# Loading x as runs of 112 consecutive rows in a fused causal convolution and SoLU layer

## The chip, the cores and the metric

The kernel runs on one core of a Trainium2 chip, in one launch. A core has four compute engines, each with its own queue of instructions that it works off strictly in order: TensorE (PE, matrix products into PSUM), VectorE (DVE), ScalarE (ACT) and GpSimd (POOL). A fifth queue, SyncE (SP), computes nothing: here it issues all DMAs, in order, and the DMAs run on 16 DMA engines. Engines wait for each other through semaphores. The metric is the device time of one execution in microseconds, the median over runs.

## The reference

x has 8 sequences of 4160 tokens with 192 features. Each of 8 heads (24 features) takes a causal convolution over 7 tokens with softmax weights, zero ahead of a sequence's first token. The result goes, token by token, through a feed-forward layer with 1024 hidden features.

```python
x_pad = np.concatenate([np.zeros((B, 6, D)), x], axis=1)
out = np.einsum('hk,bskhg->bshg', softmax(weight), windows_of_7(x_pad))
x = out.reshape(B * S, D)                       # 33280 tokens x 192
h = x @ w_in                                    # 192 -> 1024
solu = h * softmax(h)
ln = (solu - mean(solu)) / sqrt(var(solu) + 1e-6) * g_ln
return ln @ w_out                               # 1024 -> 192
```

## The kernel before

**Tiles.** The 33280 tokens are 260 tiles of 128. For each tile PE makes ph (128 x 1024, L815 and L838) from the convolved and transposed tokens yT; DVE takes the row minimum of the scaled ph (L869), ACT the exponential (L876), DVE the product (L886), ACT a half-precision copy p (L894) and the squares (L898), POOL the rest that the copy left out (L906). SP then issues a DMA that transposes p to pT (L908), PE multiplies pT by w_out into po (L938), five tiles after the tile's own ph, DVE brings po to SBUF (L948), POOL scales the rows (L1017), and SP stores them (L1030).

**Chunks.** The convolution works on chunks of 16 or 18 tiles (the first three chunks, `Chunk`, have another shape and are not touched by the change). Class `Strips` holds the other 14. A chunk's x comes in four loads (`load`, j = 0 to 3) into two SBUF tiles, one for the first half of the chunk's tokens ("late" 0) and one for the second ("late" 1). Even chunks and odd chunks use two sets of such tiles: one is named xs in the profile, the other xr. A load fetches strips of 48 rows: 32 tokens and the 16 ahead of them. 48 rows go to partitions 0 to 47 (half 0) or 64 to 111 (half 1), and 16 such strips, 64 tokens apart, lie side by side (18 in the last two chunks). Partitions 48 to 63 and 112 to 127 of these tiles are filled with zeros once, at the start (`clear`, L453: two DMAs for each of the four tiles).

**The maximum.** `sum_squares` (L376) is a reduction on DVE that takes the largest magnitude over all 128 partitions of half the strips of one tile, four per chunk. The convolution needs a scale, worked out from these four. Since a reduction reads both halves, it needs two loads to have landed.

**The first tokens of a sequence.** Where a strip starts with a sequence's first token, its 16 rows ahead belong to another sequence. `load` zeroes them with a memset on POOL right after it issued the load (L364); this memset waits for the load to land. It happens seven times, each time in xs.

**The product.** `product` (L400) runs, for each of two heads, eight matmuls of 48 rows by 32 output columns. They use both row halves of the array and its four column groups, so that all eight stand beside each other.

**The order.** It is written by hand. From tile 8 on, `three_steps` emits three tiles at a time: at the head of a step come the step's loads, then PE's products; a first "peak" (the maximum) stands on DVE ahead of the step's first row minimum L869, further ones at the end of the step. `chores` says at which tile k of chunk ch what is due: convolutions of chunk ch+1 at k = 0, 3, 6, 9; loads of chunk ch+3 at 12, 13 and 15, its fourth load at k = 1 of the next chunk; the four maxima of chunk ch+2 at 1, 4, 7 and 10. The lines are:

```python
if c2:
    fixed("load", (1, 2, 4, 5) if late else (-1, -1, -1, 1), [(c2, j) for j in range(4)])
    fixed("peak", (7, 8, 10, 12) if late else (1, 4, 7, 10), ...)
if c3:
    fixed("load", [q + late for q in (12, 13, 15 - late)], [(c3, j) for j in range(3)])
```

As 16 tiles are no multiple of three, the steps stand differently in each chunk; every third chunk they stand alike.

Of the kernel before, what the change touches and what calls it, by code (L numbers as in the profile page):

```python
# [9 lines left out]
F32 = mybir.dt.float32  # L10
# [9 lines left out]
def kernel(  # L20
# [34 lines left out]
    ROWS = HALO + Q  # L55

# [44 lines left out]
    def total(parts, name, bank=None):  # L101

        n = parts.shape[1]
        if bank is None:
            bank = single(f"pt_{name}")
        nc.tensor.matmul(
            bank[:, 512 - n : 512], ones, parts, start=True, stop=True
# [29 lines left out]
    class Chunk:  # L137
# [84 lines left out]

        def square_peaks(self):

            if self.peaks < self.cols:
                q = self.part[:, self.peaks : self.cols]
                act.activation(q, q, AF.Square, scale=16.0)

        def add_up(self, bank=None):
            self.tp = total(self.part[:, 0 : self.cols], f"x{self.ch}", bank)  # L230
# [99 lines left out]
    class Strips(Chunk):  # L330


        def __init__(self, ch):
# [3 lines left out]
            self.np, self.convs = 4, 0  # L337
# [6 lines left out]
        def place(self, j):  # L344
            half, late = j % 2, j // 2
            return half, late, strips[(self.ch - OLD) % 2][late][:, 0 : self.nt, :]

        def load(self, j):

            half, late, t = self.place(j)  # L350
            self.raw[j] = t
            assert self.ch < OLD + 2 or chunks[self.ch - 2].convs == 4
            nt, own = self.nt, slice(64 * half, 64 * half + ROWS)
            first = self.t0 + late * nt * P // 2 + Q * ((half + late) % 2) - HALO
            nc.sync.dma_start(
                t[own],
                bass.AP(
                    tensor=x.tensor, offset=first * D,
                    ap=[[D, ROWS], [2 * Q * D, nt], [1, D]],
                ),  # L360
            )
            for w in range(nt):
                if (first + HALO + 2 * Q * w) % S == 0:
                    pool.memset(t[64 * half : 64 * half + HALO, w, :], 0.0)  # L364

        def halves(self, j):
            late, n = j // 2, self.nt // 2
            return [(2 * late, j, j % 2 * n, (j % 2 + 1) * n)]

        def sum_squares(self, j, col, a, z):  # L370
            if self.part is None:
# [3 lines left out]
            self.sums += 1  # L375
            dve.tensor_reduce(  # L376
                self.part[:, col : col + 1], self.raw[j][:, a:z, :], AX.XY,
# [6 lines left out]
        def product(self, h, n, a, z, bank=None):  # L384
# [9 lines left out]
            for j in range(n):  # L394
                for half, c in STRIPS:
                    late, own = (half + c) % 2, slice(64 * half, 64 * half + ROWS)
                    raw = strips[(self.ch - OLD) % 2][late][own, 0 : self.nt, :].rearrange(
                        "p (t g) d -> p g t d", g=2
                    )
                    nc.tensor.matmul(  # L400
                        pc[late][Q * c : Q * (c + 1), :, j * HD : (j + 1) * HD],
                        taps[own, h + j, 64 * half : 64 * half + Q],
                        raw[:, c // 2, :, (h + j) * HD : (h + j + 1) * HD],
# [1253 lines left out]
```

## Time and profile before

| | us |
|---|---|
| three runs | 1296.66, 1298.22, 1305.03 |
| median | 1298.22 |
| the profiled execution, its own time | 1300.94 |
| its span, first to last instruction | 1299.2 |
| its PE clock, mean granted share | 0.955 |

All rows of the profile are of that one execution. A row of a group has its busy time, the mean of one in ns and the idle time of its engine ahead of it with what ended it. A row of a window has the busy time and count of each engine in a stretch, then the granted PE clock, the share of time that DMA packets took (of 16 engines; over 1 where packets overlap) and the GB/s moved. A row of the timeline has start, duration, engine, line, operation and, in brackets, the idle time ahead of it and what ended that. A DMA on SP's queue shows the time to issue it, not to run it.

### The profile page before, as it was taken

What the parts mean: (1) busy time and instruction counts of PE and PEld (TensorE: products, weight loads), DVE (VectorE), ACT (ScalarE), POOL (GpSimd) and SP (SyncE); (2) the same over time, 40 slices, a digit from 0 to 9 for tenths busy, and PEclk for the clock granted to TensorE, in tenths of its full rate; (3) what the DMA queues carried; (4) which work ended last, traced back from release to release, by engine and by line L of the source; (5) the groups of instructions that cost most, each with busy time, mean ns of one, the idle gap of its engine ahead of it and who ended that gap; (6) DMA issues with size and microseconds to landing.
All of it is one profiled execution on the core that took longest, in us unless ns stands there. A gap on an engine that the chain in (4) does not pass through costs nothing.

```text
span 1299.2 us, 24145 instructions
## 1 busy us (share of the span) xinstructions
PE 1154.4 (89%) x8854; PEld 665.9 (51%) x8854; DVE 994.1 (77%) x1736; ACT 954.8 (73%) x1613; POOL 756.3 (58%) x748
## 2 busy tenths in 40 slices
PE   5967877997989899798989979899896989999998
PEld 3644434554545455455445545455463555555556
DVE  8865666877868797787858868687886768878777
ACT  7954656786868688687767858677785777888786
POOL 3615453684656654766655746557556465676674
PEclk9997889998989999899989989899998899999999
DMA  8689999999999999999999999999999999999988
GB/s 230 124 125 163 151 195 177 201 174 189 195 182 204 172 201 183 179 196 187 204 159 185 188 181 196 171 195 188 183 198 156 193 179 194 201 162 182 184 148 181
DMA packets 736181, 235.69 MB, mean 181 GB/s; under 512 B 649230, under 2 KB 734654, under 8 KB 736062
## 3 DMA queue, kind: packets, MB, share of 16 engines
q1 hardware_dynamic: 736062, 234.15, 103.6%
q8 instruction: 69, 1.13, 0.4%
q14 instruction: 50, 0.41, 0.1%
HBM read 40.50 MB, written 25.56 MB: 51 GB/s over the span
## 4 chain that ended last, share of the span: by engine, by line
PE 42%; DMA 17%; POOL 15%; issue 12%; DVE 7%; ACT 4%; SPq 3%; DVEq 0%; POOLq 0%; ACTq 0%
PE po L938 20%; PE ph L815 17%; POOL p L906 10%; DMA pT<-p 9%; DMA xs<-in_x_dram 4%; DVE ph L869 3%; DMA xr<-in_x_dram 3%; PE ph L838 2%; SPq L908 2%; PE pc L400 2%; POOL raw L1017 2%; ACT p L894 2%; POOL t L1009 2%; DVE y L287 1%; DVE e L886 1%
## 5 line engine op out<-in xcount | busy, mean ns | idle before, releaser
L906 POOL TENSOR_TENSOR p<-e,p 128x1024 f16<-128x1024 f32 x257 | 546.8, 2135 | 387.2 <-ACT p L894 378.9
L938 PE MATMUL po<-ohl,pT 128*128 128x192 f16 (+1 forms) x4264 | 573.2, 293 | 119.5 <-DMA pT<-p 67.7
L938 PEld LDWEIGHTS <-pT 128*128 128x128 f16 x4264 | 397.0, 101 | 303.3 <-DMA pT<-p 85.0
L815 PE MATMUL ph<-whi,yT 128*128 128x512 f16 x1548 | 421.4, 381 | 3.8 <-DVE e L886 2.6
L876 ACT ACTIVATE e<-ph,sm 128x1024 f32<-128x1024 f32 x260 | 289.6, 1114 | 178.6 <-DVE ph L869 143.1
L886 DVE SCALAR_TENSOR_TENSOR e<-ph,cv,e 128x1024 f32<-128x1024 f32 x259 | 331.4, 1280 | 61.7 <-ACT e L876 61.0
L869 DVE TENSOR_SCALAR_CACHE_REDUCE ph<-ph,cv 128x1024 f32<-128x1024 f32 x259 | 332.8, 1287 | 35.6 <-PE ph L838 27.6
L894 ACT CAST p<-e 128x1024 f16<-128x1024 f32 x257 | 266.7, 1038 | 69.8 <-DVE e L886 50.2
L815 PEld LDWEIGHTS <-yT 128*128 128x128 f16 x2064 | 193.1, 98 | 238.1 <-issue 40.4
L898 ACT ACTIVATE sq<-e 128x1024 f32<-128x1024 f32 x260 | 274.1, 1054 | 0.2
L948 DVE TENSOR_REDUCE raw<-po 128x192 f32<-128x384 f32 x247 | 137.0, 555 | 71.5 <-PE po L938 71.4
L815 PE MATMUL ph<-wlo,yT 128*128 128x512 f16 x516 | 154.6, 382 | 0.0
L278 ACT ACTIVATE y<-pc,s 128x384 f16<-128x384 f32 (+7 forms) x158 | 72.3, 518 | 76.5 <-PE pc L400 60.9
L287 DVE SCALAR_TENSOR_TENSOR y<-pc,s,y 128x384 f16<-128x384 f32 (+7 forms) x158 | 82.0, 537 | 55.1 <-ACT y L278 54.7
L1017 POOL TENSOR_SCALAR raw<-raw,t 128x192 f32<-128x192 f32 x240 | 99.0, 425 | 0.0
L838 PE MATMUL ph<-wlo,yT 64*128 64x512 f16 x269 | 74.1, 380 | 0.6 <-DMA yT<-y 0.6
L376 DVE TENSOR_REDUCE xa<-xs 128x1 f32<-128x1536 f32 (+1 forms) x28 | 49.5, 1773 | 30.1 <-DMA xs<-in_x_dram 21.7
L376 DVE TENSOR_REDUCE xa<-xr 128x1 f32<-128x1536 f32 (+1 forms) x28 | 49.6, 1773 | 29.0 <-DMA xr<-in_x_dram 29.0
L838 PE MATMUL ph<-wlo,y 64*128 64x512 f16 x251 | 68.5, 380 | 1.5 <-DMA y<-yT 1.5
L364 POOL MEMSET xs<- 16x192 f32 x7 | 1.7, 247 | 103.7 <-DMA xs<-in_x_dram 92.1
L1009 POOL TENSOR_TENSOR t<-t,mhalf 128x8 f32<-128x8 f32 (+2 forms) x33 | 53.5, 1622 | 2.6
L876 ACT ACTIVATION_READ_ACCUMULATOR e<-ph,sm 128x1 f32 x260 | 50.1, 193 | 0.0
(142 smaller groups left out, 482.3 us busy)
## 6 DMA issues: line engine op xcount, KB each, us to landing
out_dram<-raw SPq DMA_DIRECT2D x127, 192.0 KB, 3.0
xs<-in_x_dram SPq DMA_DIRECT2D x24, 576.0 KB, 8.7
xr<-in_x_dram SPq DMA_DIRECT2D x24, 576.0 KB, 8.4
pT<-p SPq DMA_TRANSPOSE x263, 4.6
y<-yT SPq DMA_DIRECT2D x12, 256.0 KB, 3.4
xr<-in_x_dram SPq DMA_DIRECT2D x6, 480.0 KB, 5.8
xs<-in_x_dram SPq DMA_DIRECT2D x4, 648.0 KB, 9.0
xr<-in_x_dram SPq DMA_DIRECT2D x4, 648.0 KB, 8.6
```

What stands on the lines that cost most here:

```text
L376: dve.tensor_reduce(self.part[:, col : col + 1], self.raw[j][:, a:z, :], AX.XY, ALU.max, apply_absolute_value=True,)
L815: nc.tensor.matmul(bank, lhs, w[:, r, n * 512 : (n + 1) * 512], start=start and j == 0, stop=stop and j == len(ops) - 1,)
L838: nc.tensor.matmul(banks_of(t)[n], y[q, t.off : t.off + P], wlo[q, 1, n * 512 : (n + 1) * 512], start=start, stop=not start,)
L869: dve.tensor_scalar(t.ph, t.ph, t.cv[:, 0:1], None, ALU.mult, ALU.min, accum_out=t.bias)
L876: act.activation(t.e, t.ph, AF.Exp, bias=t.bias, scale=-1.0, accum_out=grp.z[:, g : g + 1])
L886: dve.scalar_tensor_tensor(t.e, t.ph, t.cv[:, 3:4], t.e, ALU.mult, ALU.mult, accum_out=t.grp.s1[:, t.g : t.g + 1],)
L894: act.copy(t.p16[:, :, 0, :], t.halves)
L898: act.activation(junk, t.e, AF.Square, accum_out=t.grp.s2[:, t.g : t.g + 1])
L906: eng.tensor_tensor(t.p16[:, :, 1, :], t.halves, t.p16[:, :, 0, :], ALU.subtract)
L938: nc.tensor.matmul(t.po[:, 0:n], t.pT[:, a, :], w, start=j == 0, stop=j == len(ops) - 1)
L948: dve.tensor_reduce(t.grp.raw[:, t.g, :], t.po[:, 0 : 2 * D].rearrange("p (a d) -> p d a", a=2), AX.X, ALU.add,)
L1017: pool.tensor_scalar(o, o, u, 1.0, ALU.mult, ALU.mult)
```

## The change

The loads of `Strips` change their shape. One load now takes 112 consecutive rows (`SPAN`) to partitions 0 to 111 at one go, and the next 112 rows start 128 tokens on. Rows 0 to 47 of such a run are one strip, rows 64 to 111 the strip 64 tokens later; rows 48 to 63 are x's rows between them, and no longer zeros. A chunk of 16 tiles has loads of 8, 8, 9 and 9 runs. The second class (late 1) starts 64 tokens earlier and has one run more, so that its row half 1 serves the strips that half 0 serves in the first class: all eight places in the array are still in use. The end of x doesn't fill a run: there two loads are cut, and their last run is zeroed first (a DVE memset that the DMA waits for).

With it go the fills (`clear`) and their eight DMAs; the maximum reads 112 partitions and one load alone; its four columns hold 8, 8, 9 and 9 tiles' worth; the first rows of a sequence are zeroed on DVE directly ahead of that load's maximum, no longer on POOL. Loads of chunk ch+3 are due at 13 and 14, its other two at k = 0 and 1 of the next chunk; the maxima at 3, 6, 8 and 10.

```diff
     class Strips(Chunk):
+        rows = SPAN
...
         def load(self, j):
 
-            half, late, t = self.place(j)
-            self.raw[j] = t
...
-            first = self.t0 + late * nt * P // 2 + Q * ((half + late) % 2) - HALO
+            late, q = divmod(j, 2)
+            m = self.nt // 2
+            n = m + late
+            self.raw[j] = t = strips[(self.ch - OLD) % 2][late][:, q * n : (q + 1) * n]
+            first = self.t0 + Q * q - HALO + late * (m * P - P // 2)
+            rows = min(SPAN, B * S - first - (n - 1) * P)
+            part = rows < SPAN
+            if part:
+                dve.memset(t[:, n - 1, :], 0.0)
+                nc.sync.dma_start(
+                    t[0:rows, n - 1, :],
...
             nc.sync.dma_start(
-                t[own],
+                t[0:SPAN, 0 : n - part],
                 bass.AP(
                     tensor=x.tensor, offset=first * D,
-                    ap=[[D, ROWS], [2 * Q * D, nt], [1, D]],
+                    ap=[[D, SPAN], [P * D, n - part], [1, D]],
                 ),
             )
-            for w in range(nt):
-                if (first + HALO + 2 * Q * w) % S == 0:
-                    pool.memset(t[64 * half : 64 * half + HALO, w, :], 0.0)
+            self.starts[j] = [
+                t[64 * half : 64 * half + HALO, w, :]
+                for half in range(2) for w in range(n)
+                if (first + 64 * half + HALO + P * w) % S == 0
+            ]
 
         def halves(self, j):
-            late, n = j // 2, self.nt // 2
-            return [(2 * late, j, j % 2 * n, (j % 2 + 1) * n)]
+            return [(j, j, 0, self.nt // 2 + j // 2)]
...
             self.sums += 1
+            for t in self.starts[j]:
+                dve.memset(t, 0.0)
             dve.tensor_reduce(
-                self.part[:, col : col + 1], self.raw[j][:, a:z, :], AX.XY,
+                self.part[0:SPAN, col : col + 1], self.raw[j][0:SPAN, a:z, :], AX.XY,
...
-                for half, c in STRIPS:
-                    late, own = (half + c) % 2, slice(64 * half, 64 * half + ROWS)
...
+                for q, late, half in STRIPS:
+                    own, skip = slice(64 * half, 64 * half + ROWS), late * (1 - half)
+                    c = Q * (2 * (half ^ late) + q)
                     nc.tensor.matmul(
-                        pc[late][Q * c : Q * (c + 1), :, j * HD : (j + 1) * HD],
+                        pc[late][c : c + Q, :, j * HD : (j + 1) * HD],
                         taps[own, h + j, 64 * half : 64 * half + Q],
-                        raw[:, c // 2, :, (h + j) * HD : (h + j + 1) * HD],
+                        self.raw[2 * late + q][
+                            own, skip : skip + m, (h + j) * HD : (h + j + 1) * HD
+                        ],
...
-    STRIPS = [(0, 0), (1, 1), (0, 2), (1, 3), (0, 1), (1, 0), (0, 3), (1, 2)]
+    STRIPS = [(q, late, half) for q in range(2) for late in range(2) for half in range(2)]
...
-    def clear(k, late):
-
-        for half in range(2):
-            nc.sync.dma_start(
-                strips[k][late][64 * half + ROWS : 64 * (half + 1)],
-                zero.unsqueeze(1).broadcast_to([64 - ROWS, NTM, D]),
             )
...
-                fixed("load", (1, 2, 4, 5) if late else (-1, -1, -1, 1), [(c2, j) for j in range(4)])
-                fixed("peak", (7, 8, 10, 12) if late else (1, 4, 7, 10),
+                fixed("load", (1, 2, 4, 5) if late else (-1, -1, 0, 1), [(c2, j) for j in range(4)])
+                fixed("peak", (7, 8, 10, 12) if late else (3, 6, 8, 10),
...
-                fixed("load", [q + late for q in (12, 13, 15 - late)], [(c3, j) for j in range(3)])
+                fixed("load", (13, 14), [(c3, 0), (c3, 1)])
```

Where instructions move. SP's queue near the end of chunk 4 (tiles 58 to 61), before. The names are the tiles above: pT with its transpose, xs with a load, out_dram with a store; "48x16x192" is partitions, strips and features.

```order
L908 DMA_TRANSPOSE pT_3434<-p_58_3431 128x16x128
L355 DMA xs_419<-in_x_dram 48x16x192 x2
L1030 DMA out_dram<-raw_2733 128x2x192
L908 DMA_TRANSPOSE pT_3503<-p_59_3500 128x16x128
L908 DMA_TRANSPOSE pT_3535<-p_60_3532 128x16x128
L908 DMA_TRANSPOSE pT_3574<-p_61_3571 128x16x128
L355 DMA xs_420<-in_x_dram 48x16x192
```

The same place in the changed kernel:

```order
L912 DMA_TRANSPOSE pT_3424<-p_58_3421 128x16x128
L366 DMA xs_417<-in_x_dram 112x8x192
L1034 DMA out_dram<-raw_2723 128x2x192
L912 DMA_TRANSPOSE pT_3491<-p_59_3488 128x16x128
L912 DMA_TRANSPOSE pT_3523<-p_60_3520 128x16x128
L912 DMA_TRANSPOSE pT_3562<-p_61_3559 128x16x128
L366 DMA xs_417<-in_x_dram 112x8x192
L366 DMA xs_418<-in_x_dram 112x9x192
```

For this chunk the loads come two, one and one before, and one, two and one now (the last is further on). In the other two standings of the steps they are two and two now. The transposes keep their order among each other.

DVE at the turn to the fourth chunk (tile 32), before. raw<-po is L948 of the text above, xa is the maximum, y the convolution's result on its way out of PSUM, ph the row minimum:

```order
L948 TENSOR_REDUCE raw_1875<-po_2007 128x192
L376 TENSOR_REDUCE xa_2075<-xs_419 128x1
L287 SCALAR_TENSOR_TENSOR y_73<-pc_6_0_2034,s_1846,y_73 128x8x48
L869 TENSOR_SCALAR ph_2025,sm_2078<-ph_2025,cv_1186 128x1024
L287 SCALAR_TENSOR_TENSOR y_73<-pc_6_1_2035,s_1846,y_73 128x8x48
L869 TENSOR_SCALAR ph_2052,sm_2083<-ph_2052,cv_1186 128x1024
```

In the changed kernel, from the same row minimum on (the two rows ahead of it are raw<-po and y, with no maximum between them):

```order
L873 TENSOR_SCALAR ph_2014,sm_2065<-ph_2014,cv_1178 128x1024
L290 SCALAR_TENSOR_TENSOR y_73<-pc_6_1_2024,s_1836,y_73 128x8x48
L873 TENSOR_SCALAR ph_2041,sm_2070<-ph_2041,cv_1178 128x1024
L890 SCALAR_TENSOR_TENSOR e_2068,s_32_1989<-ph_2014,cv_1178,e_2068 128x1024
L952 TENSOR_REDUCE raw_1863<-po_2081 128x192
L890 SCALAR_TENSOR_TENSOR e_2072,s_32_1989<-ph_2041,cv_1178,e_2072 128x1024
L873 TENSOR_SCALAR ph_2042,sm_2137<-ph_2042,cv_1178 128x1024
L952 TENSOR_REDUCE raw_1863<-po_2120 128x192
L890 SCALAR_TENSOR_TENSOR e_2139,s_32_1989<-ph_2042,cv_1178,e_2139 128x1024
L952 TENSOR_REDUCE raw_1863<-po_2153 128x192
L389 MEMSET xs_417 16x192
L390 TENSOR_REDUCE xa_2222<-xs_417 112x1
```

The maximum that stood ahead of tile 32's row minimum now stands a step (three tiles) later, with the memset that POOL had directly ahead of it.

POOL at the same turn, before (raw<-raw,t is L1017, cv the scales that the row minimum reads):

```order
L906 TENSOR_TENSOR p_28_1849<-e_1838,p_28_1849 128x2x512
L364 MEMSET xs_419 16x192
L1017 TENSOR_SCALAR raw_1480<-raw_1480,t_16_1039 128x192 x2
L906 TENSOR_TENSOR p_29_1921<-e_1914,p_29_1921 128x2x512
L218 TENSOR_SCALAR cv_1847<-cv_1847 128x1 x3
```

And changed:

```order
L910 TENSOR_TENSOR p_28_1839<-e_1828,p_28_1839 128x2x512
L1021 TENSOR_SCALAR raw_1470<-raw_1470,t_16_1031 128x192 x2
L910 TENSOR_TENSOR p_29_1909<-e_1902,p_29_1909 128x2x512
L219 TENSOR_SCALAR cv_1837<-cv_1837 128x1 x3
L910 TENSOR_TENSOR p_30_1942<-e_1906,p_30_1942 128x2x512
```

POOL's queue is the same but for the memset, which is gone from between two tiles' L906.

More of the change, by code (lines that the diff above doesn't have):

```diff
@@ L55 @@
     ROWS = HALO + Q
+    SPAN = 64 + ROWS
     QS = 2.0**-14
@@ L106, in total @@
         nc.tensor.matmul(
-            bank[:, 512 - n : 512], ones, parts, start=True, stop=True
+            bank[:, 512 - n : 512], ones[0 : parts.shape[0]], parts, start=True, stop=True
         )
@@ L336, in __init__ @@
             self.nt = self.n // P
[L337 removed]
+            self.np, self.convs, self.starts = 4, 0, [[]] * 4
             self.raw = [None] * self.np
@@ L492 @@
     act.activation(rebias[0:1], rebias[0:1], AF.Copy)
-    zero = cp.tile([64 - ROWS, D], F32, name="zero")
-    pool.memset(zero, 0.0)
     mhalf = cp.tile([P, 1], F32, name="mhalf")
@@ L1384, in three_steps @@
         soon = i == FIRST // P * 2 + 1
-        for q in work.get("clear", []):
-            clear(*q)
         if not start:
```

30 lines of the change are left out of this document (12 added, 18 removed).

## The prediction

> **What bounds the kernel.** I read the page's busy shares first, then stretches of the loop as windows, then the waits, and for each wait the timeline.
>
> ```profile
> PE 1154.4 (89%) x8854; PEld 665.9 (51%) x8854; DVE 994.1 (77%) x1736; ACT 954.8 (73%) x1613; POOL 756.3 (58%) x748
> DMA  8689999999999999999999999999999999999988
> ```
>
> PE leads, but not by enough to be the whole answer, and DMA is busy in nearly every slice. Two stretches tell what stands beside PE: the main loop with loads of x, and the first stretch behind the last load. The first fence is all engines, the second L876 alone, two records per tile.
>
> ```profile
> 229.00:1144.00 915.00, 834.37 (x6550) 473.14 (x6549) 714.93 (x1212) 682.37 (x1140) 554.58 (x547) 0.96 1.08 186
> 1144.00:1206.00 62.00, 61.87 (x484) 35.16 (x483) 48.66 (x84) 52.10 (x85) 43.06 (x41) 1.00 0.98 181
> ```
>
> ```profile
> 229.00:1144.00 915.00, 231.38 (x384) 0.96 1.08 186
> 1144.00:1206.00 62.00, 18.08 (x30) 1.00 0.98 181
> ```
>
> The main loop does 192 tiles in 915.00 us, 4.77 each; behind the loads it is 15 tiles in 62.00, 4.13 each, with PE busy 61.87 of them at full clock. Tile work costs 192 x 4.133 = 793.6 us when nothing stalls, so the main loop loses 121.4 us: 80.6 as PE's idle time, the rest mostly as slower matmuls (clock 0.96). Where? Steps at the turn of a chunk, as windows (first, a middle one, last, and the sum of all eleven), and one such step at the end, without loads:
>
> ```profile
> 280.12:302.67 22.55, 14.78 (x119) 8.18 (x118) 12.10 (x24) 10.82 (x18) 9.49 (x13) 0.89 1.15 190
> 593.26:609.72 16.46, 13.18 (x114) 7.41 (x113) 11.79 (x20) 11.40 (x21) 10.15 (x12) 1.00 1.16 171
> 1058.93:1077.55 18.62, 14.57 (x115) 8.06 (x113) 12.09 (x20) 11.48 (x21) 10.53 (x12) 0.91 1.23 178
> sum 227.79, PE 165.64 PEld 92.44 DVE 132.96 ACT 122.34 POOL 125.33; mean PE 15.06 PEld 8.40 DVE 12.09 ACT 11.12 POOL 11.39
> ```
>
> ```profile
> 1130.54:1144.05 13.51, 13.51 (x116) 7.68 (x115) 10.48 (x23) 11.16 (x19) 9.80 (x13) 1.00 0.95 149
> ```
>
> 227.79 - 11 x 13.51 = 79.2 us of the 121.4 lie in these eleven steps. The timeline of the first, and the memset of the turn before it:
>
> ```profile
> 287.94 1.32 SPq L355 DMA_DIRECT2D xr<-in_x_dram  x2
> 289.96 8.83 SPq L908 DMA_TRANSPOSE pT<-p  x1
> ...
> 299.03 1.75 DVE L376 TENSOR_REDUCE xa<-xr 128x1 f32<-128x1536 f32 x1 [9.28 <-DMA xr<-in_x_dram]
> ```
>
> ```profile
> 301.36 1.92 PE L938 MATMUL po<-ohl,pT 128*128 128x384 f16 x7 [7.46 <-DVE y L287]
> ```
>
> ```profile
> 221.46 0.25 POOL L364 MEMSET xs<- 16x192 f32 x1 [13.17 <-DMA xs<-in_x_dram]
> ```
>
> Three things happen. DVE stands 9.28 us at a maximum whose loads were issued 11 us before, PE idles 7.46 us behind it; in xs chunks POOL stands at the memset, and the L906 behind it feeds a transpose; and the transpose behind two loads takes 8.83 us to issue. In the steps at 593 and 1058 only the third occurs: they lose 2.95 and 5.11 us, the other nine 7.9 each. The wait list of the whole run:
>
> ```profile
> POOL xs L364 <- DMA xs<-in_x_dram: 92.1, 6, 25.9
> ...
> PE po L938 <- DMA pT<-p: 67.7, 32, 10.1
> ...
> DVE xa L376 <- DMA xr<-in_x_dram: 29.0, 4, 9.7
> ...
> DVE xa L376 <- DMA xs<-in_x_dram: 21.7, 3, 10.0
> ```
>
> **The change, part by part.**
>
> *The waits.* The memsets leave POOL. The first maximum moves from k = 1 to 3 and needs one load, issued two steps (25 us) earlier instead of two loads one step earlier. The landings of a load in the trace, fastest, median and slowest:
>
> ```profile
> DMA to landing us min/median/max: 6.8/8.6/13.3
> ```
>
> Against 13.3 us both waits end. Late next is the third cause, the transposes.
>
> *The loads.* A chunk's rows go from 3072 to 3808 (8, 8, 9 and 9 runs of 112). What a row costs depends on the shape. Windows in which almost only x was moved: 48-partition loads (first two lines), 128-partition loads of the first chunks, and two zero fills of 16 partitions with a load's start:
>
> ```profile
> DMA packets 1471, 1.12 MB, mean 160 GB/s; under 512 B 23, under 2 KB 1470, under 8 KB 1470
> ```
>
> ```profile
> DMA packets 1089, 0.82 MB, mean 137 GB/s; under 512 B 19, under 2 KB 1089, under 8 KB 1089
> ```
>
> ```profile
> DMA packets 1697, 1.28 MB, mean 319 GB/s; under 512 B 36, under 2 KB 1697, under 8 KB 1697
> ```
>
> ```profile
> DMA packets 522, 0.39 MB, mean 92 GB/s; under 512 B 33, under 2 KB 522, under 8 KB 522
> ```
>
> The rate rises with the partitions: 92, 149 (mean of the two), 319 GB/s. A straight line from 48 to 128 partitions gives 285 at 112. Four loads of 589,824 B cost 4 x 3.96 = 15.8 us per chunk before; 2 x 688,128 and 2 x 774,144 B at 285 cost 2 x 2.41 + 2 x 2.72 = 10.3. That saves 5.5 us of DMA time per chunk, though 24% more bytes move. Bounds: 149 GB/s as now (19.6 us, 3.8 more per chunk) and 319 (9.2 us). I take the line since 112 lies nearer to 128 than to 48, and the fills follow the same trend without HBM.
>
> The Trainium skill (SBUF — State Buffer, Door 1: The DMA port swizzle) says that DMA speed goes by how many of 16 ports the partitions reach. By its table 48 partitions put a sixth of the bytes on each of four ports, 112 at most a fourteenth on any. By it alone the loads would run 14/6 times as fast, 348 GB/s by estimate and 8.4 us a chunk; no burst would be left over, and the sum would come to about 1156. The trace agrees on 48 against 128 partitions in direction (149 against 319 GB/s), while the rule's own ratio there is 16/6 = 2.7, not 2.1.
>
> *Bursts that stay.* Two bursts a chunk remain ahead of transposes, now 4.8 and 5.4 us where a pair took 7.9 and lost 2.95. The loss lies between 0 (the shorter burst is covered by the five tiles between a tile's ph and its po) and 2.95; I take the middle, 1.5, so 24 x 1.5 = 36 us of the 121.4 stay (0 to 71).
>
> *Maxima two in a step.* In two of three standings k = 6 and 8, or 8 and 10, fall in one step.
>
> ```profile
> L376 DVE TENSOR_REDUCE xa<-xr 128x1 f32<-128x1536 f32 x24 | 41.9, 1744 | 29.0 <-DMA xr<-in_x_dram 29.0
> ...
> L376 DVE TENSOR_REDUCE xa<-xs 128x1 f32<-128x1728 f32 x4 | 7.8, 1946 | 10.0 <-DMA xs<-in_x_dram 10.0
> ```
>
> ```profile
> 255.97:268.69 12.72, 12.72 (x112) 7.30 (x111) 11.58 (x19) 11.07 (x20) 8.51 (x12) 1.00 0.95 163
> ```
>
> A step with one maximum has DVE busy 11.58 of 12.72 us; 1.74 more makes 13.3, 0.6 over, in 8 of 12 chunks: 5 us stay. The 0.2 us by which a maximum of nine runs is longer fits into the 1.1 us that is free, as do seven memsets on DVE of some 0.22 us (the one below has their shape). If that cover goes, they cost 7 us.
>
> ```profile
> 0.89 0.22 DVE L160 MEMSET xr<- 16x192 f32 x1 [0.89 <-PEq L1643]
> ```
>
> *The product.* The eight matmuls' order changes, not their count or size; each still has a place of its own.
>
> ```profile
> L400 PE MATMUL pc<-xs,taps 48*32 48x192 f32 x768 | 22.4, 329 | 1.1 <-DVE raw L948 1.0
> L400 PE MATMUL pc<-xr,taps 48*32 48x192 f32 x768 | 21.7, 329 | 0.2 <-DVE raw L948 0.2
> ```
>
> 768 x 329 ns in 22.4 us busy: eleven deep, so they overlap whichever column group comes next. Cost 0. The two cut loads at the end let SP wait for a DVE memset: DVE runs about a step ahead of SP at such turns (at 299.03 - 9.28 = 289.7 it had come to a maximum that stands a step behind the loads that SP issued at 287.94), so cost 0.
>
> *The start.* Tiles 8 to 31:
>
> ```profile
> 67.44:229.00 161.56, 119.48 (x869) 70.16 (x868) 101.79 (x176) 91.27 (x160) 67.75 (x73) 0.87 1.02 163
> 207.38:229.03 21.65, 14.60 (x119) 8.26 (x118) 12.09 (x24) 11.19 (x20) 8.33 (x13) 0.85 1.11 168
> ```
>
> ```profile
> xs<-zero SPq DMA_DIRECT2D x4, 216.0 KB, 5.6
> xr<-zero SPq DMA_DIRECT2D x4, 216.0 KB, 5.3
> ```
>
> ```profile
> 80.27 4.38 SPq L355 DMA_DIRECT2D xs<-in_x_dram  x2
> 94.57 1.71 SPq L908 DMA_TRANSPOSE pT<-p  x1
> ```
>
> 24 x 4.133 = 99.2, so 62 us are lost here. The transpose at 94.57 waited for POOL, which stood at the memset of these loads until 91.6; without it SP could go on at 84.65: 10 us. The turn at 207 loses 8.1 and gets back 7. Eight fills of 221,184 B at 92 GB/s are 19 us of DMA time; half on the path is 9 (0 to 19). Together 26, bounds 10 and 45.
>
> *Sum.* 121.4 - 36 - 5 + 26 = 106.4 us. The profiled execution took 1300.94 (span 1299.2 and 1.7 around it): 1194.5. It lies 2.7 above the median of 1298.2, so the forecast for a median is 1192. With both lower bounds (71 stay, 10 at the start) the gain is 55, with both upper ones 161: 1243 and 1137.
>
> **Rivals.**
>
> *Slower: a row costs what it costs now.* If strided reads of 768 B and not the partitions set the 149 GB/s, each chunk needs 3.8 us more of DMA time; as DMA is busy in nearly every slice, this comes on top: 14 x 3.8 less 19 for the fills is +34, 1332, and the waits that go give nothing back since the transposes wait instead. It turns where 3808 rows take as long as 3072, at 185 GB/s. For it: packets fill all slices, share 1.08. Against it: 92 GB/s for fills that touch no HBM, 319 for rows of the same 768 B. The Trainium skill (DMA: Bandwidth & Descriptors, Anatomy of one DMA) has a fit of 2 us plus bytes at 436 GB/s, stated for another issuing path; by bytes alone the loads become dearer, which is on this rival's side, but at that rate a load of 589,824 B would take 1.35 us, and the rows above give 3.96.
>
> *DMA is the bound and the rate rises halfway*, to 217 GB/s: 13.5 us per chunk, 2.3 saved; 12 x 2.3 + 5 + 19 = 52, so 1246. For it: the same DMA line. Against: steps at full PE with the same share (1.16 at 593, 0.98 behind the loads).
>
> *The burst takes the wait's place.* If the waits only hid what the transposes lose, each of 24 bursts keeps the mean of 2.95 and 5.11, 4.0: 97 stay, the gain is 121 - 97 - 5 + 26 = 45, 1253. Against: bursts become shorter.
>
> *The array takes no two halves of one column group in a row.* L400's busy time (22.4 + 21.7) doubles, 1236. Against: eleven deep now.
>
> **Chances.** My forecast 0.62, halfway 0.15, burst 0.12, columns 0.03, slower 0.08. The forecast's own range is 1150 to 1230; to leave out no more than two in ten it must take in halfway and burst, so 1150 to 1258. A measurement of this kernel tells about 1% (13 us) from no change. Only the slower rival and mixtures near it reach there: faster 0.89, same 0.05, slower 0.06.
>
> **What would show it.** L364 is gone from the waits and xa no longer waits for loads; x loads land in 5 to 6 us; turns of a chunk take 14 to 15 us; the main loop's 192 tiles take about 835 us, DMA share falls below 1.08, PE's clock rises over 0.96. The forecast is wrong if loads still move at 150 GB/s, or if PE po waits for pT more than the 67.7 us in which it did so far.

## The result, and the profile after

| | us |
|---|---|
| before, four runs | 1296.66 to 1305.03, median 1298.05 |
| after, four runs | 1207.24 to 1215.65, median 1211.24 |
| ratio | 0.9322, 95% interval 0.9272 to 0.9372 |
| the profiled execution after | 1208.76 (span 1207.1) |

The change made the kernel 6.8% faster, 87 us. The forecast was 1192 with a range of 1150 to 1258: the total lies in the range, and the gain is 19 us smaller than forecast. Profile against profile it is 1300.94 - 1208.76 = 92.2 us where the sum had 106.4. One of the four runs of experiment e7 took 5282.84 us, its others 1198.75 to 1207.50; it isn't counted.

The first two rows are from the page of the changed kernel, busy time by engine and DMA's busy share in 40 slices:

```profile
PE 1130.8 (94%) x8854; PEld 653.1 (54%) x8854; DVE 997.9 (83%) x1746; ACT 954.9 (79%) x1613; POOL 754.7 (63%) x740
...
DMA  7799999999999999999999999999999999989888
```

PE has gone from 89% to 94% of a shorter span; DMA is as full as it was. The two stretches of the prediction, tiles 8 to 31 and the main loop's 192 tiles, as windows of the changed kernel:

```profile
68.35:194.41 126.06, 112.36 (x865) 67.18 (x864) 99.01 (x176) 90.98 (x160) 69.47 (x72) 0.95 1.02 193
194.41:1052.82 858.41, 815.78 (x6555) 462.59 (x6554) 721.48 (x1222) 682.77 (x1141) 551.40 (x540) 1.00 1.10 208
```

Tiles 8 to 31 went from 161.56 to 126.06, a gain of 35.5 where the sum had 26. The main loop went from 915.00 to 858.41, a gain of 56.6 where it had 80. PE's clock is 1.00 (0.96 before), and DMA's share rose from 1.08 to 1.10, though it was forecast to fall. The turn from chunk 3 to 4 and the step behind it:

```profile
263.26:280.25 16.99, 13.36 (x115) 7.37 (x114) 11.79 (x20) 11.37 (x21) 9.72 (x10) 1.00 1.10 220
280.25:294.44 14.19, 12.81 (x110) 6.95 (x108) 11.89 (x20) 10.66 (x18) 7.16 (x5) 1.00 1.16 222
```

The turn still loses 3.6 us of PE's time, and the step behind it 1.4. What PE waits for there (PEld is its loading of weights), from the list of waits of the whole run (total, times, longest), and the group of the maximum (its last number is DVE's idle time ahead of it):

```profile
PEld L942 <- DMA pT<-p: 69.5, 49, 6.4
...
PE po L942 <- DMA pT<-p: 51.1, 38, 6.2
```

```profile
L390 DVE TENSOR_REDUCE xa<-xs 112x1 f32<-112x1728 f32 (+2 forms) x28 | 52.3, 1874 | 0.2
```

No maximum waits for a load any more (0.2 us is all, and 0.0 for xr), and no memset: the two waits that the change was to end are gone. PE's wait for the transposed tiles pT went only from 67.7 to 51.1. SP's queue at the same turn shows why (start, duration of the issue):

```profile
272.82 0.97 SPq L366 DMA_DIRECT2D xr<-in_x_dram  x2
273.84 1.78 SPq L1034 DMA_DIRECT2D out_dram<-raw  x1
275.73 6.13 SPq L912 DMA_TRANSPOSE pT<-p  x1
```

The transpose behind two loads takes 6.13 us to issue; it took 8.83 at this turn before. This is what is left, and the experiments ask what it is made of.

### The profile page after: what moved, and what is told of

It is laid out like the page before. It is cut to its first block, busy times and chain, and to the rows that moved or that the text cites. A ratio compares the mean times of both kernels' runs of the same rounds, so it can differ in the third digit from the quotient of the medians.

```text
span 1207.1 us, 24073 instructions
## 1 busy us (share of the span) xinstructions
PE 1130.8 (94%) x8854; PEld 653.1 (54%) x8854; DVE 997.9 (83%) x1746; ACT 954.9 (79%) x1613; POOL 754.7 (63%) x740
## 4 chain that ended last, share of the span: by engine, by line
PE 40%; POOL 19%; issue 12%; DMA 10%; DVE 10%; ACT 6%; SPq 3%; POOLq 0%; DVEq 0%; ACTq 0%
PE po L942 19%; PE ph L819 16%; POOL p L910 12%; DMA pT<-p 9%; DVE ph L873 5%; ACT p L898 2%; POOL raw L1021 2%; PE pc L412 2%; POOL t L1013 2%; SPq L912 2%; PE ph L842 2%; DVE e L890 2%; DVE y L290 1%; ACT y L281 1%; ACT e L880 1%
## 5 line engine op out<-in xcount | busy, mean ns | idle before, releaser
L942 PE MATMUL po<-ohl,pT 128*128 128x192 f16 (+1 forms) x4264 | 551.1, 286 | 55.7 <-DMA pT<-p 51.1
L942 PEld LDWEIGHTS <-pT 128*128 128x128 f16 x4264 | 384.5, 99 | 228.6 <-DMA pT<-p 69.5
L390 DVE TENSOR_REDUCE xa<-xs 112x1 f32<-112x1728 f32 (+2 forms) x28 | 52.3, 1874 | 0.2
L390 DVE TENSOR_REDUCE xa<-xr 112x1 f32<-112x1728 f32 (+2 forms) x28 | 52.4, 1871 | 0.0
L902 ACT ACTIVATION_READ_ACCUMULATOR sq<-e 128x1 f32 x260 | 50.0, 192 | 0.0
```

What stands on the lines that cost most here:

```text
L390: dve.tensor_reduce(self.part[0:SPAN, col : col + 1], self.raw[j][0:SPAN, a:z, :], AX.XY, ALU.max, apply_absolute_value=True,)
L902: act.activation(junk, t.e, AF.Square, accum_out=t.grp.s2[:, t.g : t.g + 1])
L942: nc.tensor.matmul(t.po[:, 0:n], t.pT[:, a, :], w, start=j == 0, stop=j == len(ops) - 1)
```

## The experiments

Every ratio is to the kernel before, run on the same chip, with its 95% interval; three rounds each. In two of the kernels part of the input is left out.

**e1: the memset alone.** The kernel before, with the seven memsets on DVE right ahead of the maximum, as the change has them.

```diff
-                    pool.memset(t[64 * half : 64 * half + HALO, w, :], 0.0)
+                    self.starts.append((late, w, t[64 * half : 64 * half + HALO, w, :]))
...
+            for late, w, t in self.starts:
+                if late == j // 2 and a <= w < z:
+                    dve.memset(t, 0.0)
             dve.tensor_reduce(
```

> The kernel before, with one thing changed: the seven memsets of a sequence's first rows go from POOL to DVE, directly ahead of the maximum that reads them. Loads, fills and due times stay. Theory (three causes share the loss: waits on landings, the loads' own DMA time, fills): POOL no longer stands at the memset (92.1 us of waiting gone), but DVE still stands at the first maximum of the same loads, so only part comes back: about 10 us at the start and some 3 us in four of the six xs turns, 1270 to 1285. Rival 'POOL's memset is most of it': below 1250. Rival 'DMA time is all of it': 1290 to 1300.

Measured: 1286.34, ratio 0.9918 (0.9894 to 0.9943), 11 us faster. That is just short of what was expected. DVE now stands where POOL stood: it waits 62.8 us for loads in all, 50.7 before.

**e2: both waits, old loads.** e1 with the changed kernel's due times, so that loads come earlier and maxima later; loads keep their 48 partitions, and the fills stay.

```diff
-    fixed("load", (1, 2, 4, 5) if late else (-1, -1, -1, 1), ...)
-    fixed("peak", (7, 8, 10, 12) if late else (1, 4, 7, 10),
+    fixed("load", (1, 2, 4, 5) if late else (-1, -1, 0, 1), ...)
+    fixed("peak", (7, 8, 10, 12) if late else (3, 6, 8, 10),
...
-    fixed("load", [q + late for q in (12, 13, 15 - late)], [(c3, j) for j in range(3)])
+    fixed("load", (13, 14), [(c3, 0), (c3, 1)])
```

> As the run before it in this list, and in addition the due times of the changed kernel (maxima at 3, 6, 8, 10; loads 13, 14, then 0, 1). So both waits on landings go, while loads stay 48 rows by 16 strips and the fills stay. Theory: xa and xs wait for no load any more, but each of 24 bursts keeps what a burst of the old loads costs without a wait (2.95 to 5.11 us, 4.0 in the mean): 1250 to 1270, so the shape of the loads and the fills are worth the other 40 to 60 us down to 1211. Rival 'the waits are all of it': 1205 to 1225. Rival 'DMA is the bound, waits only showed it': 1285 to 1300.

Measured: 1285.25, ratio 0.9909 (0.9882 to 0.9936). My theory missed; the rival's number came out. In its list of waits DVE's are down to a third (50.7 us before), and PE's for pT has grown from 67.7:

```profile
PE po L942 <- DMA pT<-p: 81.6, 40, 6.6
...
PE po L942 <- DVE y L287: 16.0, 5, 4.1
...
DVE xa L380 <- DMA xs<-in_x_dram: 9.0, 2, 4.9
DVE xa L380 <- DMA xr<-in_x_dram: 8.5, 2, 4.7
```

So with the old loads, the end of the waits by itself is worth 1%, not the better part of the gain. Beside e1, where only the due times differ, PE's wait for y, which DVE brings behind its maximum, falls from 54.1 to 16.0, and its wait for pT grows from 51.9 to 81.6: most of the stall moves from DVE's wait into PE's wait for a transpose.

**e3: the new loads cut in two.** The changed kernel, with each load as two DMAs, to partitions 0 to 63 and 64 to 111. Same bytes, same rows, fewer partitions at a time.

```diff
-            nc.sync.dma_start(
-                t[0:SPAN, 0 : n - part], ...
+            for p, z in ((0, 64), (64, SPAN)):
+                nc.sync.dma_start(
+                    t[p:z, 0 : n - part], ...
```

> The changed kernel with each load issued as two, partitions 0 to 63 and 64 to 111: the same rows, addresses, pitch and bytes. Theory (the rate goes by the partitions that one DMA reaches): by the line from 48 to 128 partitions, 64 move 183 and 48 move 149 GB/s, so the four loads of a chunk take some 17.6 us and not 10.3; bursts as long as before, 1260 to 1310. Rival 'the rate comes from the pitch between runs or the bytes in a row': the rate stays near 285 GB/s, and the time within 10 us of 1211.

Measured: 1269.31, ratio 0.9802 (0.9762 to 0.9842): 58 of the 87 us are given back with nothing changed but the partitions that one DMA covers, and twice the number of DMAs.

**e4: no loads.** The changed kernel without the loads of the ten chunks 5 to 14; their input is left out.

```diff
+            if self.ch >= OLD + 2 and self.nt == 16:
+                return
```

> The changed kernel without the loads of ten of the fourteen strip chunks (chunks 5 to 14 of 16 tiles): their convolutions and maxima read what chunks 3 and 4 left in the tiles, so part of the input is left out. Theory: what the main loop still loses against clean tile work (about 65 us over 192 tiles) is what bursts of loads do to the transposes behind them; ten of twelve such chunks lose it no more: 1150 to 1165. Rival 'what is left is DVE with two maxima in a step, or PE's own order': 1195 or more.

Measured: 1170.45, ratio 0.9025 (0.9002 to 0.9048), somewhat above what was expected. The stretch of tiles 80 to 175 (six chunks, in each of which one chunk's loads are due) as a window of this kernel, and then of the changed kernel:

```profile
395.91:799.32 403.41, 403.18 (x3278) 232.44 (x3277) 357.07 (x607) 340.89 (x571) 275.73 (x270) 1.00 0.97 176
```

```profile
410.27:836.36 426.09, 407.78 (x3278) 231.42 (x3277) 359.48 (x610) 341.14 (x570) 275.69 (x270) 1.00 1.10 209
```

Without loads PE is busy 403.18 of 403.41 us: nothing else stalls it there. A tile then costs 403.41 / 96 = 4.202 us, not the 4.133 of the stretch at the program's end, which has no maxima and fewer convolutions. The loads cost the changed kernel 22.7 us here, 3.8 a chunk.

**e5: the old due times.** The changed kernel with loads and maxima due when they were before (the same lines as in e2, the other way).

> The changed kernel with the due times of before: of a chunk's four loads three at k = 12, 13, 15 and one at k = 1, maxima at 1, 4, 7 and 10. Theory (what the loads cost in DMA time decides, and the early maximum by itself is worth little): 1211 to 1226, DVE waits for loads of x again but PE's wait for pT falls by about as much. The prediction's account (the waits are what the main loop lost): the waits come back with about 40 of the 80 us it credited them and their bursts with, 1240 to 1260.

Measured: 1209.89, ratio 0.9330 (0.9287 to 0.9373), the changed kernel's own ratio within the interval. Its waits:

```profile
PE po L942 <- DMA pT<-p: 34.9, 34, 5.6
...
PE po L942 <- DVE y L290: 17.6, 6, 3.9
...
DVE xs L389 <- DMA xs<-in_x_dram: 12.0, 3, 4.6
...
DVE xa L390 <- DMA xr<-in_x_dram: 7.9, 2, 4.3
```

DVE waits 20 us again and PE's wait for pT is 16 us shorter; in its place PE waits 17.6 us for DVE's y, 4.0 in the changed kernel. In sum PE waits 52.5 us here and 55.1 there. The two waits are the same DMA time seen from two engines; the due times, as the change set them, brought nothing measurable.

**e6: another queue for the loads.** The changed kernel with the strips' loads issued by ScalarE.

```diff
-            nc.sync.dma_start(
+            nc.scalar.dma_start(
                 t[0:SPAN, 0 : n - part],
```

> The changed kernel with the loads of the strips issued by ScalarE, on its own DMA queue, all else as it is. Theory A (the transposes lose time because they stand behind whole loads in SP's one queue): most of the 62 us that stay in the main loop go, 1155 to 1190, and PE's wait for pT falls from 51 to under 20 us. Theory B (a load takes the 16 DMA engines and the queue does not matter): 1205 to 1220, PE's wait for pT stays near 51. If ScalarE is held up where it issues a load, more: 1220 to 1250.

Measured: 1248.67, ratio 0.9613 (0.9566 to 0.9660), 37 us slower than the changed kernel, in the third of the expected bands. From its timeline, all engines, at the turn to chunk 4:

```profile
254.63 1.60 ACTq L366 DMA_DIRECT2D xr<-in_x_dram  x2
...
258.05 9.20 SPq L912 DMA_TRANSPOSE pT<-p  x1
...
269.82 3.80 PE L942 MATMUL po<-ohl,pT 128*128 128x384 f16 x16 [6.10 <-DMA pT<-p]
...
269.87 7.89 ACTq L366 DMA_DIRECT2D xr<-in_x_dram  x2
...
277.82 1.05 ACT L281 ACTIVATE y<-pc,s 128x384 f16<-128x384 f32 x2 [6.92 <-DMA pT<-p]
```

The loads stand in another queue, and the transpose still takes 9.20 us to issue: SP's queue is not what holds it up. The Trainium skill (DMA: Bandwidth & Descriptors, Issuing engines are not separate DMA queues) says that DMAs issued from ScalarE and SyncE run on the same 16 DMA engines and interleave; this run agrees. ScalarE moreover is held up itself. The 7.89 us of the second pair are not time to issue: either load takes 0.32, and in the 7.26 between them ScalarE stands, since the second load waits for a semaphore that comes only with the landing of a transpose of p (the 6.92 of the last row). The trace has three such stands, of 7 to 8 us.

**e7: one load to a step.** The changed kernel, no two loads in a row.

```diff
-    fixed("load", (1, 2, 4, 5) if late else (-1, -1, 0, 1), ...)
+    fixed("load", (1, 2, 4, 5) if late else (-1, -1, 2, 5), ...)
...
-    fixed("load", (13, 14), [(c3, 0), (c3, 1)])
+    fixed("load", (12 + late, 15), [(c3, 0), (c3, 1)])
```

> The changed kernel with one load to a step of three tiles (due at 12, 15, 2 and 5) in place of two loads in each of two steps, maxima as they are. Theory (a burst costs what of it is longer than some slack of 2 to 2.5 us, so two of 2.4 to 2.7 us in a row cost 2.6 and one alone about 0.3): 48 x 0.3 = 14 stay of 62, so 1155 to 1180. Rival (the cost goes by bytes, however they are dealt out): 1203 to 1217.

Measured: 1199.81 (the middle of three runs), ratio 0.9257 (0.9204 to 0.9311), beside 0.9272 to 0.9372 for the changed kernel: the intervals overlap, so a small gain is possible, and the 30 to 55 us of my theory are out. PE's idle time was for the most part not a matter of two loads in a row: over tiles 80 to 175 it is 15.4 us here and 18.3 in the changed kernel.

No run e8 was made. What putting the memsets back on POOL costs is read from e10 against e5.

**e9: the fills alone.** The changed kernel with the eight fills of before at their places in SP's queue (to partitions 112 to 127, which nothing reads).

```diff
+    def clear(k, late):
+        for half in range(2):
+            nc.sync.dma_start(
+                strips[k][late][SPAN:P, 0:NTM],
+                zero.unsqueeze(1).broadcast_to([64 - ROWS, NTM, D]),
+            )
```

> The changed kernel with the eight fills of before at their old places in SP's queue; they write partitions 112 to 127 of the strips' tiles, which nothing reads. The prediction's term: half of 19 us on the path, 9, so 1220 (bounds 0 and 19: 1211 to 1230). Rival: they cost more than their DMA time since they come in pairs ahead of transposes, 1230 to 1240.

Measured: 1232.68, ratio 0.9502 (0.9457 to 0.9548): 21 us over the changed kernel, in the rival's band (23 by the ratios, and their intervals leave some 9 either way, so the total may still lie inside the prediction's bounds of 0 and 19). Its windows, tiles 8 to 31 and the main loop, and two of the four pairs of fills in SP's queue:

```profile
67.36:218.35 150.99, 120.78 (x865) 70.67 (x864) 99.20 (x176) 91.22 (x160) 69.57 (x72) 0.89 0.97 176
218.35:1076.43 858.08, 816.94 (x6555) 463.96 (x6554) 720.98 (x1222) 683.01 (x1140) 552.35 (x540) 0.99 1.10 208
```

```profile
63.42 5.32 SPq L467 DMA_DIRECT2D xs<-zero  x2
...
80.43 4.71 SPq L467 DMA_DIRECT2D xs<-zero  x2
```

All of it lies in tiles 8 to 31 (150.99 beside 126.06); the main loop is the same to 0.3 us. SP stands some 5 us at a pair, and what is behind it is late by that. But much of this is the experiment's own. Both fills of a pair write partitions 112 to 127, so SP holds the second until the first has landed; its list of waits has

```profile
SPq L467 <- DMA xs<-zero: 7.0, 2, 3.5
SPq L467 <- DMA xr<-zero: 6.9, 2, 3.5
```

which is 13.9 us over the four pairs. In the kernel before, the two fills go to different partitions, and SP goes on at once:

```profile
78.98 1.25 SPq L453 DMA_DIRECT2D xs<-zero  x2
```

So the 21 us are the price of fills with that wait in it. What they cost in the kernel before can't be read from this run, and the rival's band came out for a reason of the experiment's own.

**e10: loads' shape and fills alone.** e5 with the memsets back on POOL, right behind the load. Of what the change did against waits, the due times and the memsets are undone; a maximum still needs one load and not two.

```diff
+            for s in self.starts[j]:
+                pool.memset(s, 0.0)
...
-            for t in self.starts[j]:
-                dve.memset(t, 0.0)
```

> The changed kernel with the due times of before and with the memsets back on POOL right behind the load: of the change only the loads' shape and the missing fills stay. Theory (only DMA time counts): 1209 to 1220, so close to 1211 though all that was done against waits is undone. Rival (POOL's memset costs what moving it brought in the kernel before, 12): 1219 to 1230, with POOL waiting for xs some 10 us each time.

Measured: 1232.85, ratio 0.9505 (0.9482 to 0.9528). My theory missed, and the rival's band is passed by 3: the memset on POOL costs 23 us beside e5, more than the 11 of e1. It costs them in the main loop: from the first ph matmul of tile 35 to that of tile 227 it is 878.6 us here and 854.6 in e5, from tile 8 to tile 35 143.9 and 143.1. One of the eight that this kernel has, in a row each from the timelines of SP, POOL, SP and PE:

```profile
611.53 0.87 SPq L366 DMA_DIRECT2D xs<-in_x_dram  x1
...
617.55 0.25 POOL L379 MEMSET xs<- 16x192 f32 x1 [11.33 <-DMA xs<-in_x_dram]
...
620.03 7.06 SPq L912 DMA_TRANSPOSE pT<-p  x3
...
624.56 5.38 PE L942 MATMUL po<-ohl,pT 128*128 128x384 f16 x32 [4.96 <-DMA pT<-p]
```

POOL stands 11.33 us until the load has landed. The p that it owes comes after the memset, so SP has no transpose to issue from the end of a store at 613.1 to 620.0: the DMA engines idle behind the load (DMA's share is 0.93 from 613 to 617 and 0.03 from 617 to 620), then PE waits 4.96 us. This wait is not DMA time seen from elsewhere, it adds to it, and so it was worth ending.

**e11: e7 with maxima at 1, 4, 7 and 10**, so that no step has two.

```diff
-    fixed("peak", (7, 8, 10, 12) if late else (3, 6, 8, 10),
+    fixed("peak", (7, 8, 10, 12) if late else (1, 4, 7, 10),
```

> One load to a step (due at 12, 15, 2 and 5), and maxima at 1, 4, 7 and 10, so that no step has two. Theory: the 8 us of one load to a step and the 3 us of the steps with two maxima add up, 1197 to 1203. Rival (the early maximum waits again, as loads are now further on): 1204 to 1215.

Measured: 1210.45, ratio 0.9333 (0.9312 to 0.9355); the rival's band. Its waits for loads are back:

```profile
DVE xa L390 <- DMA xr<-in_x_dram: 13.5, 7, 3.8
DVE xs L389 <- DMA xs<-in_x_dram: 11.8, 3, 5.1
```

**e12: runs of 128 rows.** The changed kernel, each load with 128 rows to all partitions; 16 of them serve nothing, 14% more bytes.

```diff
-                t[0:SPAN, 0 : n - part],
+                t[0:P, 0 : n - part],
...
-                    ap=[[D, SPAN], [P * D, n - part], [1, D]],
+                    ap=[[D, P], [P * D, n - part], [1, D]],
```

> The changed kernel with runs of 128 rows to all 128 partitions in place of 112; the 16 further rows are read by nothing, 14% more bytes. Theory A (a load's time goes by rows per partition, whatever their number over 100, as 319 GB/s at 128 beside 285 at 112 says): 1207 to 1217, landings as in the changed kernel. Theory B (it goes by bytes at 285 GB/s): 14 chunks x 1.5 us more DMA time, 1225 to 1235.

Measured: 1195.90, ratio 0.9218 (0.9195 to 0.9241), below both bands. It moves more and is 15 us faster than the changed kernel (intervals apart). It beats both kernels. The runs of a load now also follow each other in x without a gap, where the changed kernel skips 16 rows between them; no run tells this apart from the number of partitions. Tiles 80 to 175 of it:

```profile
404.44:824.68 420.24, 406.15 (x3278) 230.69 (x3277) 359.31 (x610) 341.19 (x571) 275.80 (x270) 1.00 1.10 218
```

**e13: half the loads' rows.** The changed kernel, in the ten chunks 5 to 14 only the first four runs of each load; the other runs are left out.

```diff
+            m = n - part if self.ch < OLD + 2 or self.nt > 16 else n // 2
...
-                t[0:SPAN, 0 : n - part],
+                t[0:SPAN, 0:m],
```

> The changed kernel with only the first half of the runs of each load fetched, in ten chunks of 16 tiles; the other half of these chunks' input is left out. Theory (a chunk has room for some 6.5 us of loads, only what is over it is lost: 9.3 lost of 15.8, 3.8 lost of 10.3): about 5 us fit, 1170 to 1178, as without any loads (1170). Rival (the loss goes by the DMA time of the loads, 37% of it): half way, 1187 to 1195.

Measured: 1169.71, ratio 0.9012 (0.8993 to 0.9031), as without any loads. Tiles 80 to 175 take 403.68 us, e4 took 403.41. The theory's number: half the loads cost nothing, the other half all.

**What the loads cost, by their DMA time.** In the middle of a pair of loads no transpose is under way, so the rate of the loads can be read there (a store of 0.2 MB may be among them). One such window each, of e2, e3, the changed kernel and e12:

```profile
DMA packets 1063, 0.80 MB, mean 146 GB/s; under 512 B 17, under 2 KB 1063, under 8 KB 1063
```

```profile
DMA packets 1842, 1.39 MB, mean 198 GB/s; under 512 B 58, under 2 KB 1841, under 8 KB 1841
```

```profile
DMA packets 1721, 1.30 MB, mean 260 GB/s; under 512 B 29, under 2 KB 1721, under 8 KB 1721
```

```profile
DMA packets 1762, 1.34 MB, mean 335 GB/s; under 512 B 18, under 2 KB 1762, under 8 KB 1762
```

Over all pairs of tiles 32 to 205 the means are 145, 195, 261 and 338 GB/s; other cuts of the middle give 142 to 151, 182 to 195, 248 to 262 and 307 to 338. A chunk's bytes (2.36 MB in e2, 2.92 in e3 and the changed kernel, 3.34 in e12, 1.38 in e13, taken at 261) over these rates give the DMA time of a chunk's loads; the loss per chunk is the time of tiles 80 to 175 over e4's 403.41, divided by six. The last column is the DMA time less the loss. All five have the memset on DVE and the same due times.

| kernel | tiles 80 to 175, us | DMA time of a chunk's loads, us | lost per chunk, us | difference |
|---|---|---|---|---|
| e2, 48 partitions | 457.13 | 16.3 | 9.0 | 7.3 |
| e3, 64 and 48 | 450.06 | 15.0 | 7.8 | 7.2 |
| changed, 112 | 426.09 | 11.2 | 3.8 | 7.4 |
| e12, 128 | 420.24 | 9.9 | 2.8 | 7.1 |
| e13, 112, half | 403.68 | 5.3 | 0.0 | |

About 7 us of loads fit into a chunk of 67 us for nothing (7 to 8 by the other cuts); every microsecond over that is a microsecond of the kernel. That is a bound by DMA time, and it holds across the shapes, bytes and numbers of DMAs tried. Not all of the loss is PE standing still: in e2 PE is busy for 422.00 us there, 18.8 more than in e4, at a clock of 0.96 beside 1.00.

## Why the prediction was right, and where it was not

**The total** is in the range and the direction is right. Of its terms three were mis-sized, and they partly cancel: 106.4 + 9.5 (start) - 15.6 (bursts) - 8.2 (yardstick and maxima) = 92.1, which is the profiled difference. The main loop alone was 24 us too high; that the start made up for 9.5 of it is luck.

**The loads' rate: right.** "A straight line from 48 to 128 partitions gives 285 at 112", 10.3 us per chunk. The middle of the bursts gives 261 and 11.2; the 15.8 of before is 16.3. The saving of 5.5 us per chunk is 5.1. The rival by which a row costs what it did falls with this. One reading in it is wrong: the 14/6 for 112 and the 16/6 = 2.7 for 128 against 48 partitions are not the cited rule's own ratios, but what comes out when the port with the most rows sets the pace. By the number of ports reached (16 and 8, see the last section) the ratio is 2 for either; for 128 the prediction's rows gave 2.1, and here it is 338 / 145 = 2.3.

**"Against 13.3 us both waits end": they did, and that was worth less than the text lets one think.** The chain of runs splits the 87 us: from before to e10 some 64 us are the loads' shape, the missing fills and the maximum's need of one load, from e10 to e5 23 are the memset on DVE, and from e5 to the changed kernel, the due times, none. The other way round, e1 and e2 have the waits' end at 11 and 1 with the old loads. DVE's wait at the first maximum was next to no cost of its own, POOL's at the memset was. Of the three causes that the prediction put side by side, two were the same DMA time.

**"Two bursts a chunk remain ... I take the middle, 1.5": mis-sized.** The main loop after takes 858.4; 192 tiles at e4's 4.202 are 806.8. The 51.6 between them are 24 bursts of 2.15. The reason given for a low value, that five tiles between ph and po cover the shorter burst, does not hold: e7's single loads, half as long, stall nearly as much in sum (tiles 80 to 175 take 423.6 there, 426.1 in the changed kernel, 403.4 without loads). What a burst costs is not its length less a cover of its own, but the chunk's whole load time less 7 us.

**"192 x 4.133 = 793.6 us when nothing stalls": too low by 13.2,** since the stretch it is from lacks work that the main loop has (e4, above). So 13.2 of what the prediction put down to slower matmuls was work. The 5 for steps with two maxima stood for part of this.

**The start: 26, measured 35.5: a term was missing.** The sum had 10 for the memset, 7 for the turn and 9 for the fills ("half on the path"), and nothing for the loads' own shorter time, which counts here too. From the first ph matmul of tile 8 to that of tile 35 the kernel before takes 174.8 us, e1 168.6, e2 168.1, e3 151.8 and the changed kernel 140.1. So the memset, from before to e1, is worth 6 of the 17 that stood for it and for the turn. From e3 to the changed kernel, where only the cut of the loads differs, it is 12: the missing term. The 16 between e2 and e3 hold the fills together with the rest that tells these two apart (loads of 16.3 and 15.0 us a chunk, a maximum that needs one load). What the fills cost in the kernel before stays open: e9's 24.9 in its window have up to 13.9 of that run's own in them, so the 9 is not refuted. The upper bound of 45 is not the sum of the terms' bounds, which is 10 + 8 + 19 = 37; the 35.5 lies below both.

**The rivals.** "DMA is the bound" had the mechanism right and the rate wrong: with the forecast's rate its sum, 12 x 5.5 + 5 + 19 = 90, would have come within 3 us of the profiled gain, if partly by luck: its 71 for the main loop is 14 too high, its 19 for the start 16 too low. I argued against it from steps that run at full PE with the same DMA share (1.16, and 0.98 behind the loads). That share counts packets that overlap and cannot tell a full DMA from one with room: it is 0.97 in e4, 1.10 in the changed kernel, and 1.05 over e13's tiles 80 to 175, where the loads cost nothing. "The burst takes the wait's place" describes e2, and is no rival of the bound but its other face. The array's column groups are out by the row of the product itself:

```profile
L412 PE MATMUL pc<-xs,taps 48*32 48x192 f32 (+1 forms) x896 | 27.0, 332 | 1.5 <-DVE raw L952 1.4
```

With 26.2 for xr that is 53.2 us busy, and before, all forms together, it was 52.1; that rival would have had it double.

**What was to be seen.** L364 and xa's wait went, and the clock rose, as said. Loads were to land in 5 to 6 us; the page has medians of 6.5 to 7.6. That a load waits behind what was issued ahead of it would explain this, but wasn't tested:

```profile
xs<-in_x_dram SPq DMA_DIRECT2D x14, 756.0 KB, 7.6
xs<-in_x_dram SPq DMA_DIRECT2D x12, 672.0 KB, 6.5
```

The turns were to take 14 to 15 us; of the two steps shown above one takes 16.99 and one 14.19. The main loop was to take 835 and takes 858; the share was to fall and rose. PE's wait for pT stayed under the 67.7 us that would have spoken against the forecast.

**What stays open.** Why the free time is 7 us a chunk and not more wasn't shown. Placing the loads in other ways (e5, e7, e11) moved the time by less than the intervals tell apart, so it isn't a matter of one bad place. How the start's 16 us split between fills and loads is open too. e3 doubles the DMAs as well as cutting the partitions; that it lies on the table's line says that the rate is enough to explain it, and no run varies the count alone.

## What to carry to other kernels

Where a DMA queue is nearly full, ask of each change how many microseconds of DMA time it takes out, and count a wait for a load as a cost only if the DMAs stand still behind it. To find out what a set of transfers costs, leave them out and halve them: the two runs show the bound, and the room under it, which the share of busy time did not. Try loads to all partitions, even where some rows serve nothing: here 128 beat 112. And look in the trace of an experiment for waits that its edit brought in: e9's price of the fills had 13.9 us of them.

## What the runs showed of the hardware

The rate of a load of 768-byte rows rose with the partitions that it covers, more steeply near the top than the line I had drawn: 145 GB/s at 48, 261 at 112 and 338 at 128, so that 128 rows take less time than 112 (9.9 beside 11.2 us per chunk) though they are 14% more bytes. The same rows and addresses in two DMAs of 64 and 48 partitions moved at 195.

The Trainium skill (SBUF — State Buffer, Door 1: The DMA port swizzle) says that DMA bandwidth depends on how many of the 16 SBUF ports the partitions reach. By its table 48 partitions reach 8 ports, 112 and 128 all 16; from the measured 338 one would estimate 169 at 48 and 338 at 112. The measured 145 is somewhat below the first, the 261 well below the second. If one takes the prediction's reading of the table instead, that the port with the most partitions (8 in all three cases) sets the pace, the estimate is 338 x 112 / 128 = 296 at 112 and 338 x 48 / 128 = 127 at 48, and the further 16 rows should be free, which e12 bears out and exceeds; the 261 is below this estimate too. Neither reading gives the 261, and no run here says why.

A load in ScalarE's queue can hold up ScalarE's own work: in e6 it stood 7.26 us between two loads that took 0.32 us each to issue, until a transpose had landed.
